# Strassen's seven products for the output layer of the last eight token tiles, in a fused retention and MLP kernel

## Chip, cores, metric

One Trainium2 chip, one core. The metric is the device time of one launch in microseconds (us), median of several runs. TensorE is PE in the profile (PEld: its weight loads), VectorE DVE, ScalarE ACT, GpSimd POOL, SyncE SP.

## The reference

Two layers follow each other. The first is a linear recurrence per batch and head with decay `gamma`; the second an MLP over all 4 x 768 = 3072 tokens with `d_model` 512 and `d_ff` 2048:

```python
for t in range(S):                      # S = 768, 4 batches, 8 heads of 64
    state = gamma * state + k[:, :, t]^T v[:, :, t]
    y[:, :, t] = scale * q[:, :, t] state
x = y as (3072 tokens, 512)
h = x @ w_in                            # 512 -> 2048
g = h + sin(alpha * h) ** 2 / (alpha + 1e-9)
out = g @ w_out                         # 2048 -> 512
```

## The kernel before

The recurrence is done in 24 chunks of 128 tokens (token tiles); a chunk's results land transposed, in bf16, in `xT`. The tiles go through the MLP in ten groups of sizes 4, 2, 2, 2, 2, 2, 2, 2, 2, 4 (`sizes`; group 0 is the first). Where a group is called g below, it is numbered 0 to 9.

The first layer of a group works in slots (class `Slot`): four matmuls with K = 128 for each block f of 128 of the 2048 hidden units write `ph` in PSUM; ScalarE takes the sine (L613) and squares it (L618), VectorE forms `s * rec_alpha + ph` (L625, `add`) and writes it in bf16 to `gT`. A group of two tiles has slots of two blocks (128x256 each, 8 slots); group 9, with four tiles, has slots of one block (128x512, 16 slots). The second layer (`ff_out`, L635) multiplies a tile's 16 blocks of `gT` by `w_out`: 16 matmuls of 512 columns into one bank `po`, which VectorE copies to SBUF (`take`, L649) and SyncE stores.

The order on each engine is the order of the code (a manual schedule). `phase(g, outs, att, ...)` writes one group: per slot n, in this order, the slot's matmuls with sine and square; what is left of the previous recurrence step (`exit`: `xT` from `py`, L494; `keep`: the state `s_f`; `hand`: its copy `s_q`); the recurrence step placed at this slot (`att`: matmuls into `py` or `y`, scores into `pa`, then the mask on VectorE, L406); a share of `outs`, which are the output matmuls of group g-1; and last the slot's `add`. Slot (g, n) below is slot n of phase g. After phase 9 the outputs of group 9 stand alone: three tiles by `ff_out`, the fourth by `last_tile`.

```python
for g in range(2, NG):
    phase(g, out_pieces(g - 1, range(sizes[g - 1])), atts[g], 4 // sizes[g], ...)
for fn in out_pieces(NG - 1, range(sizes[-1] - 1)):
    fn()
last_tile(NG - 1, sizes[-1] - 1)
```

PSUM has eight banks, in three tags: `mm`, four buffers of one bank in rotation (slots, `po`, some scores); `two`, one buffer of two banks (`py`, `y`); `pa`, one buffer of two banks (scores; the slots (6, 5) and (7, 5) as well). A tile that takes a buffer waits for the last reader of the tile before it.

Of the kernel before, what the change touches and what calls it, by code (L numbers as in the profile page):

```python
# [38 lines left out]
def kernel(  # L39
# [91 lines left out]
    def load_seq(bt, names="qkv", part=slice(None), between=None):  # L131
# [3 lines left out]
        if ("seq", bt) not in raw:  # L135
            raw["seq", bt] = (big.tile([128, nh, 2, NP, D], BF16, name=f"qk_seq{bt}"),
                              big.tile([128, nh, NP, D], BF16, name=f"v_seq{bt}"))
# [502 lines left out]
    def take(g, ts, by=None):  # L640
        o_sb = work.tile([128, d_model], F32, name="o_sb", tag="o_sb", bufs=5)
        if (g, ts) == end:
            h = d_model // 2
            nc.vector.tensor_copy(o_sb[:, :h], po[g, ts][:, :h])
            nc.scalar.copy(o_sb[:, h:], po[g, ts][:, h:])
        elif by is nc.scalar:
            nc.scalar.copy(o_sb, po[g, ts])
        else:
            nc.vector.tensor_copy(o_sb, po[g, ts])  # L649
# [2 lines left out]
        for r in (half(0), half(1)) if g == NG - 1 else (slice(0, 128),):
            nc.sync.dma_start(out=out_view[r, groups[g][ts], :], in_=o_sb[r])

    def last_tile(g, ts):

        lo = 0
        for n in (3 * d_model // 4, d_model // 4):
            c = slice(lo, lo + n)
            lo += n  # L660
            ph = psum.tile([128, n], F32, name="poh", tag="mm", bufs=4)
            for f in range(FF):
                nc.tensor.matmul(ph, gT[g][:, f, ts * C:(ts + 1) * C], w_out[:, f, c],  # L663
                                 start=(f == 0), stop=(f == FF - 1))
            o_sb = work.tile([128, d_model], F32, name="o_sb", tag="o_sb", bufs=5)[:, :n]
            if lo < d_model:
                nc.scalar.copy(o_sb, ph)  # L667
            else:
                nc.vector.tensor_copy(o_sb, ph)
            nc.sync.dma_start(out=out_view[:, groups[g][ts], c], in_=o_sb)  # L670
# [225 lines left out]

    def last_loads():
        nc.gpsimd.tensor_copy(seen, st["qkT", P[17]][:, 0, 0:1])
# [41 lines left out]
```

## Time and profile before

| | |
|---|---|
| time, median of 3 runs | 207.42 us (207.19 to 208.68) |
| profiled execution, span | 207.1 us |
| PE busy | 200.0 us, 97% of the span |
| DVE, ACT, POOL busy | 154.5, 151.9, 123.1 us (75, 73, 59%) |
| matmuls | 2383 |
| chain that ended last | PE 85%, DMA 7%, POOL 6% |

The profile gives one execution. Its groups of instructions name source line, engine, output and inputs, shapes and a count, with busy time and mean duration. The timeline has start and duration, and in brackets how long the engine had waited before and for whom. Windows are stretches of the span with each engine's busy time. An engine's instructions overlap a little: the step from one start to the next is what it can repeat.

### The profile page before, as it was taken

The page shows a single profiled execution, that of the slowest core. Times are in us where ns is not written, and L with a number is a line of the kernel's source. Part 1 is how long each engine was busy: PE and PEld are TensorE (multiplying, and loading weights), DVE is VectorE, ACT ScalarE, POOL GpSimd, SP SyncE. Part 2 cuts the span into 40 slices and gives each one's busy share as a digit, 9 for nine tenths or more (in the row PEclk, how much of TensorE's full clock was granted, in tenths as well). Part 3 has the DMA queues.
Part 4 walks back from the last instruction along what each step waited for, and adds up shares of the span by engine and source line. Part 5 has one row for each costly group of instructions (what it writes and reads, how often), then busy time and mean ns, then how long its engine had stood idle before and what let it go on. Part 6 is the DMA issues. An engine that isn't in the chain of part 4 may idle for free.

```text
span 207.1 us, 5839 instructions
## 1 busy us (share of the span) xinstructions
PE 200.0 (97%) x2383; PEld 124.8 (60%) x2383; DVE 154.5 (75%) x324; ACT 151.9 (73%) x310; POOL 123.1 (59%) x171
## 2 busy tenths in 40 slices
PE   7889999999989999999999999999999999999994
PEld 7435544557766766666766666766766654444443
DVE  4777499977999888878889695985977965656220
ACT  7768788657997787787787869688686779999000
POOL 8998986999999976899692916974220000000000
DMA  8999999999999999999997896994714101010223
GB/s 128 145 175 191 201 201 176 167 128 112 224 152 184 95 166 179 171 129 128 203 146 69 105 125 118 120 120 108 104 42 64 53 1 52 0 54 0 88 64 101
DMA packets 102810, 24.79 MB, mean 120 GB/s; under 512 B 93392, under 2 KB 99840, under 8 KB 102784
## 3 DMA queue, kind: packets, MB, share of 16 engines
q0 software_dynamic: 80080, 13.38, 93.6%
q1 hardware_dynamic: 22704, 11.06, 28.0%
q8 instruction: 18, 0.29, 0.6%
q14 instruction: 8, 0.07, 0.1%
HBM read 27.30 MB, written 6.29 MB: 162 GB/s over the span
## 4 chain that ended last, share of the span: by engine, by line
PE 85%; DMA 7%; POOL 6%; issue 0%; DVE 0%; POOLq 0%
PE po L635 38%; PE ph L610 38%; DMA w_out<-in_moe_w_out_dram 4%; DMA qkT<-qkr 3%; POOL qkr L125 3%; POOL vr L125 2%; PE poh L663 2%; PE py L372 1%; PE pt L290 1%; PE pa L387 1%; PE py L436 1%; POOL w_in L161 1%; PE py L445 1%; PE pa L394 1%; PE pa L420 1%; PE y L436 1%
## 5 line engine op out<-in xcount | busy, mean ns | idle before, releaser
L625 DVE SCALAR_TENSOR_TENSOR gT<-s,rec_alpha,ph 128x256 bf16<-128x256 f32 (+3 forms) x164 | 79.6, 522 | 27.9 <-ACT s L618 27.5
L610 PE MATMUL ph<-xT,w_in 128*128 128x256 bf16 (+3 forms) x656 | 98.3, 291 | 0.0
L613 ACT ACTIVATE s<-ph,alpha_sb 128x256 f32<-128x256 f32 (+3 forms) x164 | 76.0, 506 | 28.2 <-PE ph L610 24.7
L635 PE MATMUL po<-w_out,gT 128*128 128x512 bf16 x368 | 94.7, 380 | 0.1
L610 PEld LDWEIGHTS <-w_in 128*128 128x128 bf16 x656 | 63.2, 98 | 32.6 <-DVE s_f L568 0.5
L618 ACT ACTIVATE s<-s 128x512 f32<-128x512 f32 (+1 forms) x94 | 58.7, 625 | 2.8
L635 PEld LDWEIGHTS <-gT 128*128 128x128 bf16 x368 | 34.3, 98 | 30.2 <-DVE gT L625 0.5
L149 POOL DMA_DIRECT2D qk_seq<-in_q_dram x32 | 21.5, 704 | 4.1 <-DMA v_seq<-in_v_dram 3.9
L149 POOL DMA_DIRECT2D qk_seq<-in_k_dram x32 | 21.3, 703 | 3.6 <-DMA qk_seq<-in_q_dram 2.9
L649 DVE COPY o_sb<-po 128x512 f32<-128x512 f32 x20 | 13.8, 688 | 9.2 <-PE po L635 8.8
L149 POOL DMA_DIRECT2D v_seq<-in_v_dram x24 | 16.8, 754 | 0.0
L188 POOL TENSOR_TENSOR v_seq<-v_seq,kgq 128x512 bf16<-128x512 bf16 x9 | 9.3, 1060 | 5.9 <-DMA v_seq<-in_v_dram 5.9
L125 POOL DMA_DIRECT2D vr<-in_v_dram x11 | 10.3, 932 | 1.6 <-DMA w_in<-in_moe_w_in_dram 1.1
L406 DVE TENSOR_TENSOR aTw<-pa,maskq 128x768 bf16<-128x768 f32 x10 | 9.5, 953 | 0.0
L667 ACT COPY o_sb<-poh 128x384 f32<-128x384 f32 x1 | 0.5, 479 | 12.0 <-PE poh L663 12.0
L494 DVE TENSOR_TENSOR xT<-py,qg 128x512 bf16<-128x512 f32 x13 | 8.9, 683 | 0.5 <-PE py L452 0.5
L682 PE MATMUL spare<-warm 128*128 128x112 bf16 (+1 forms) x54 | 7.8, 316 | 1.2 <-DVE warm L198 1.2
L520 POOL CAST s_q<-s_f 128x256 bf16<-128x256 f32 x1 | 0.4, 396 | 14.2 <-DVE s_f L514 14.2
L390 DVE TENSOR_TENSOR aT<-pa,mask 128x1024 bf16<-128x1024 f32 x7 | 8.5, 1219 | 0.1
L520 ACT CAST s_q<-s_f 128x256 bf16<-128x256 f32 x12 | 4.7, 394 | 2.7 <-DVE s_f L514 2.7
L125 POOL DMA_DIRECT2D qkr<-in_q_dram x7 | 6.4, 918 | 0.3 <-DMA w_out<-in_moe_w_out_dram 0.3
L161 POOL DMA_DIRECT2D w_in<-in_moe_w_in_dram x8 | 6.2, 792 | 0.7 <-DMA w_out<-in_moe_w_out_dram 0.6
(123 smaller groups left out, 175.5 us busy)
## 6 DMA issues: line engine op xcount, KB each, us to landing
out_dram<-o_sb SPq DMA_DIRECT2D x20, 256.0 KB, 4.2
w_in<-in_moe_w_in_dram POOLq DMA_DIRECT2D x8, 256.0 KB, 8.6
w_out<-in_moe_w_out_dram POOLq DMA_DIRECT2D x8, 256.0 KB, 8.3
vr<-in_v_dram POOLq DMA_DIRECT2D x11, 128.0 KB, 5.6
v_seq<-in_v_dram POOLq DMA_DIRECT2D x16, 80.0 KB, 6.2
qkr<-in_q_dram POOLq DMA_DIRECT2D x7, 128.0 KB, 6.3
qkr<-in_k_dram POOLq DMA_DIRECT2D x7, 128.0 KB, 6.2
qk_seq<-in_q_dram POOLq DMA_DIRECT2D x16, 48.0 KB, 4.9
```

The lines of the kernel that those rows point to most:

```text
L125: nc.gpsimd.dma_start(out=t, in_=chunk_of(src, j))
L149: nc.gpsimd.dma_start(out=o, in_=src[bt, head(b, m, e), now[0] * C:(now[-1] + 1) * C, :].rearrange("(f i) d -> i f d", i=64))
L188: eng.tensor_mul(t, t, by[:, j % NCH, :, None].to_broadcast([128, H, D]))
L390: return {"mask": lambda: nc.vector.tensor_mul(aT.rearrange("p e n t -> p (e n) t"), pa.rearrange("p e (n t) -> p (e n) t", n=NP), mask_bc)}
L406: return {"mask": lambda: nc.vector.tensor_mul(aT, pa[:, :, 0:384].rearrange("p e (m t) -> p e m t", m=2), maskq[:, None, None, :].to_broa ...
L494: nc.vector.tensor_mul(o, st["pyw", old][:, :, 0:256].rearrange("p b (m t) -> p b m t", m=2), by)
L610: nc.tensor.matmul(self.ph[:, m, :], w_in[:, i, f * 128:(f + 1) * 128], xT[g][:, i, self.lo:self.hi], start=(m == 0 and i == 0), stop=(i = ...
L613: nc.scalar.activation(out=self.s[:, m, :], in_=self.ph[:, m, :], func=ACTF.Sin, scale=alpha_sb[:, f:f + 1])
L618: nc.scalar.activation(out=self.s, in_=self.s, func=ACTF.Square)
L625: nc.vector.scalar_tensor_tensor(gT[self.g][:, f, self.lo:self.hi], self.s[:, m, :], rec_alpha[:, f:f + 1], self.ph[:, m, :], op0=ALU.mult ...
L635: nc.tensor.matmul(po[g, ts], gT[g][:, f, ts * C:(ts + 1) * C], w_out[:, f, :], start=(f == 0), stop=(f == FF - 1))
L649: nc.vector.tensor_copy(o_sb, po[g, ts])
```

## The change

The output layer of group 7, group 8 and the two halves of group 9 (`fast = (7, 8, 9)`) is now computed for a pair of tiles at once, as a product of 2x2 blocks: two tiles by two halves of the hidden units, times two halves of the hidden units by two halves of the output columns. Strassen's scheme needs seven block products in place of eight. Each is 8 matmuls of 256 columns (K = 128 each), so a pair has 56 matmuls of 256 columns where it had 32 of 512.

The combined blocks are made in bf16. Those of `w_out` (`mix_w`, five combinations, 20 pieces of 128x512): 8 pieces on GpSimd, 12 on VectorE behind slots of phases 6 and 7. Those of `gT` (`mix_g`): a sum, a difference and a third sum for each pair of blocks j and j+8, behind a slot; for group 7 the first two on GpSimd and the third on VectorE, for group 8 all on GpSimd, for group 9 all on VectorE. So that j and j+8 come together, the slots of these groups take their blocks in that order. Class `Seven` holds a pair: products 5 and 2 go into bank `b`, 4 and 3 and later 7 and 6 into bank `a`, 1 into bank `c`. ScalarE copies `b` to SBUF (`hold`, `b_sb`); VectorE adds `a` and `b_sb` (`cross`: two of the four output blocks), forms `t_sb` = `c` - `b_sb` (`rest`) and adds it to `a` (`main`: the other two). The stores are 128x256.

```diff
-            self.g, self.fs = g, range(f, f + nf)
+            self.g, self.fs = g, f if isinstance(f, tuple) else range(f, f + nf)
...
+    def mix_w(eng, count=1):
+        for _ in range(count):
+            n, i = w_todo.pop(0)
+            a, b, op = W_MIX[n]
+            js = slice(2 * i, 2 * i + 2)
+            w_mix[n, i] = next(w_home)
+            eng.tensor_tensor(w_mix[n, i], w_block(*a, js), w_block(*b, js), op=op)
...
+        engs[0].tensor_tensor(ts, s0, s1, op=ALU.add)
+        engs[1].tensor_tensor(td, d0, d1, op=ALU.subtract)
+        engs[2].tensor_tensor(tx, x0, x1, op=ALU.add)
...
+        IN = {5: "b", 2: "b", 4: "a", 3: "a", 1: "c", 7: "a", 6: "a"}
...
+        def hold(self):
+            self.bsb = self.tmp("b_sb")
+            nc.scalar.copy(self.bsb, self.at["b"])
...
+        def banks(k):
+            if g < NG - 2:
+                if k == "c":
+                    return psum.tile([128, 2, 512], F32, name="c", tag="two")[:, 0, 0:NH]
+                return psum.tile([128, 2, NH], F32, name=k, tag="mm", bufs=4)
+            if k == "c":
+                return psum.tile([128, 2, 512], F32, name="c", tag="pa")[:, 0, 0:NH]
+            if "ab" not in po:
+                po["ab"] = psum.tile([128, 2, 512], F32, name="ab", tag="two")
+            return po["ab"][:, "ba".index(k)].rearrange("p (x n) -> p x n", x=2)
+        s = Seven(g, 0, banks)
+        return s.pieces((5, J), (2, J), s.hold, (4, J), (3, J), s.cross, (1, J), s.rest, (7, J), (6, J), s.main)
...
+        def far_banks(k):
+            if k == "b":
+                return near_banks(k)
+            if k == "a3":
+                return psum.tile([128, 2, 512], F32, name="a3", tag="pa")
+            if "a4c" not in po:
+                po["a4c"] = psum.tile([128, 2, 512], F32, name="a4c", tag="two")
+            return po["a4c"][:, int(k == "c"), 0:NH]
+        x, y = Seven(g, 0, near_banks), Seven(g, 1, far_banks, True)
+        todo = x.pieces((5, J0), (2, J0), (4, J0), (3, J0), (5, J1), (2, J1), x.hold, (4, J1), (3, J1), x.cross, (1, J), x.rest)
+        todo += y.pieces((5, J), (2, J), y.hold, (4, J), (3, J), y.cross)
+        todo += x.pieces((7, J), (6, J), x.main)
+        todo += y.pieces((1, J), y.rest, (7, J), lambda: y.main(7), (6, J, 0), lambda: y.main(0), (6, J, 1), lambda: y.main(1))
...
+            if g in fast and (nf == 2 or n % 2):
+                mix_g(g, n if nf == 2 else n // 2, g_by[g])
+            for fn in behind_slot.get((g, n), ()):
+                fn()
+    g_by = {7: (nc.gpsimd, nc.gpsimd, nc.vector), 8: (nc.gpsimd,) * 3, 9: (nc.vector,) * 3}
...
     def last_loads():
+        mix_w(nc.gpsimd, 3)
         nc.gpsimd.tensor_copy(seen, st["qkT", P[17]][:, 0, 0:1])
         load_seq(3, "v")
+        mix_w(nc.gpsimd, 5)
...
+    for spot in ((6, 0), (6, 2), (6, 3), (6, 6), (6, 7), (7, 0), (7, 1), (7, 2), (7, 3), (7, 5), (7, 6), (7, 7)):
+        behind_slot.setdefault(spot, []).append(lambda: mix_w(nc.vector))
     for g in range(2, NG):
-        phase(g, out_pieces(g - 1, range(sizes[g - 1])), atts[g], 4 // sizes[g], tags=tags[g], early=(6,) if g == 5 else ())
-    for fn in out_pieces(NG - 1, range(sizes[-1] - 1)):
-        fn()
-    last_tile(NG - 1, sizes[-1] - 1)
+        outs = fast_pieces(g - 1) if g - 1 in fast else out_pieces(g - 1, range(sizes[g - 1]))
+        phase(g, outs, atts[g], 4 // sizes[g], tags=tags[g], early=(6,) if g == 5 else ())
+    fast_end(NG - 1)
```

`J` is range(8), `J0` its first seven and `J1` the last. `last_tile` is gone, and the last pair's `a` is split in two banks so that its end leaves in pieces of 128 columns.

**Place one: VectorE in phase 7, from the copy of `po` in the slot before it up to the mask of the recurrence step at slot (7, 4).** Before:

```order
L649 COPY o_sb<-po 128x512
L625 SCALAR_TENSOR_TENSOR gT<-s,rec_alpha,ph 128x256 x8
L649 COPY o_sb<-po 128x512
L625 SCALAR_TENSOR_TENSOR gT<-s,rec_alpha,ph 128x256 x2
L406 TENSOR_TENSOR aTw<-pa,maskq 128x768
L568 TENSOR_TENSOR s_f<-s_f,pa 128x256
```

Now, from the copy in slot (7, 3) on (L683 is `mix_w`, L717 the third sum of `mix_g`; the slots (7, 0) to (7, 2) have the same pair behind their adds):

```order
L645 COPY o_sb<-po 128x512
L626 SCALAR_TENSOR_TENSOR gT<-s,rec_alpha,ph 128x256 x2
L717 TENSOR_TENSOR g_mix<-gT 128x128
L683 TENSOR_TENSOR w_mix<-w_out 128x512
L407 TENSOR_TENSOR aTw<-pa,maskq 128x768
L569 TENSOR_TENSOR s_f<-s_f,pa 128x256
```

Two instructions have come behind each slot's adds, and ahead of the mask and of `s_f`; GpSimd makes the other two combinations (L715, L716, 128x256 each) of the same slot at the same time.

**Place two: VectorE around the recurrence step at slot (8, 4), from that step's mask on.** Before:

```order
L406 TENSOR_TENSOR aTw<-pa,maskq 128x768
L625 SCALAR_TENSOR_TENSOR gT<-s,rec_alpha,ph 128x256 x2
L494 TENSOR_TENSOR xT<-py,qg 128x2x2x128
L514 TENSOR_TENSOR s_f<-s_f,pa 128x256
L625 SCALAR_TENSOR_TENSOR gT<-s,rec_alpha,ph 128x256 x4
```

Now (L782 is `cross`, L788 `rest`):

```order
L407 TENSOR_TENSOR aTw<-pa,maskq 128x768
L782 TENSOR_TENSOR o_sb<-a,b_sb 128x512
L626 SCALAR_TENSOR_TENSOR gT<-s,rec_alpha,ph 128x256 x2
L495 TENSOR_TENSOR xT<-py,qg 128x2x2x128
L515 TENSOR_TENSOR s_f<-s_f,pa 128x256
L788 TENSOR_TENSOR t_sb<-c,b_sb 128x512
L626 SCALAR_TENSOR_TENSOR gT<-s,rec_alpha,ph 128x256 x4
```

TensorE at the same slot, in the changed kernel, where the share of output matmuls behind the recurrence step goes over from product 3 to product 1 (with the semaphores waited for):

```order
L761 LDWEIGHTS gT
L761 MATMUL a<-w_mix,gT 128x256
L761 LDWEIGHTS g_mix [waits DVE_49]
L761 MATMUL c<-w_mix,g_mix 128x256 [waits PE_49]
L761 LDWEIGHTS g_mix
```

The first matmul of product 1 is a wait that was not there: it opens `c` in the buffer `two`, which `py` of this slot's recurrence step holds until L495 has read it. L495 stands behind `cross` and behind the adds of slot (8, 4).

**Place three: TensorE in slot (9, 4), in the changed kernel, at the end of product 2 (`ab` holds the banks `b` and `a` of group 8 in one tile).**

```order
L611 MATMUL ph<-xT,w_in 128x512
L761 LDWEIGHTS g_mix
L761 MATMUL ab<-w_out,g_mix 128x256
L761 LDWEIGHTS gT
L761 MATMUL ab<-w_mix,gT 128x256 [waits Activation_49]
L611 LDWEIGHTS w_in
L611 MATMUL ph<-xT,w_in 128x512 [waits DVE_49]
```

ScalarE at the same place:

```order
L614 ACTIVATE s<-ph,alpha_sb 128x512
L619 ACTIVATE s<-s 128x512
L769 COPY b_sb<-ab 128x512
```

Product 4 now waits for `hold` (L769), which ScalarE does behind the sine and the square of slot (9, 4); before, no output matmul of this phase waited for ScalarE but through `gT`.

More of the change, by code (lines that the diff above doesn't have):

```diff
@@ L135, in load_seq @@
         if ("seq", bt) not in raw:
[L136 to L137 removed]
+            raw["seq", bt] = (big.tile([128, nh, 2, NP, D], BF16, name=f"qk_seq{bt}", tag=f"qk_seq{bt}"),
+                              big.tile([128, nh, NP, D], BF16, name=f"v_seq{bt}", tag=f"v_seq{bt}"))
         tqk, tv = raw["seq", bt]
@@ L629 @@
     po = {}
-    end = (NG - 1, sizes[-1] - 1)
     def ff_out(g, ts, f):
@@ L641, in take @@
         o_sb = work.tile([128, d_model], F32, name="o_sb", tag="o_sb", bufs=5)
[L642 to L646, printed above, removed]
+        if by is nc.scalar:
             nc.scalar.copy(o_sb, po[g, ts])
@@ L651, in take @@
             return o_sb
[L652 to L670, printed above, removed]
+        nc.sync.dma_start(out=out_view[:, groups[g][ts], :], in_=o_sb)
@@ new lines, with w_homes @@
+    w_todo = [(n, i) for n in (1, 4, 3, 7, 6) for i in range(FH // 2)]
+    def w_homes():
+        for _ in range(11):
+            yield big.tile([128, 2, NH], BF16, name="w_mix", tag="vr", bufs=11)
+        for tag, n in (("qk_seq1", 6), ("v_seq1", 3)):
+            t = big.tile([128, n, 2, NH], BF16, name="w_mix", tag=tag)
+            for i in range(n):
+                yield t[:, i]
+    w_home = w_homes()
+    def mix_w(eng, count=1):
[5 more added lines that the diff above has]
+            eng.tensor_tensor(w_mix[n, i], w_block(*a, js), w_block(*b, js), op=op)
@@ new lines, in fast_end, with near_banks @@
+    def fast_end(g):
+        J, J0, J1 = range(FH), range(FH - 1), range(FH - 1, FH)
+        def near_banks(k):
+            if k == "c":
+                return psum.tile([128, NH], F32, name="c", tag="mm", bufs=4)
+            return psum.tile([128, 2, NH], F32, name=k, tag="mm", bufs=4)
+        def far_banks(k):
[11 more added lines that the diff above has]
+        todo += y.pieces((1, J), y.rest, (7, J), lambda: y.main(7), (6, J, 0), lambda: y.main(0), (6, J, 1), lambda: y.main(1))
+        for fn in todo:
+            fn()
```

134 lines of the change are left out of this document (131 added, 3 removed).

## The prediction

> **What bounds the kernel now.** I read the busy time by windows first, cut at the phases, then the chain of waits, then the timeline of the places that the change touches. Windows (columns: stretch, its length, busy time of PE, PEld, DVE, ACT, POOL, granted clock):
>
> ```profile
> 137.60:152.90 15.30, 15.30 (x210) 10.53 (x209) 12.04 (x26) 11.75 (x25) 6.87 (x8) 1.00 0.68 84
> 152.90:169.48 16.58, 16.58 (x258) 11.29 (x257) 12.85 (x26) 11.97 (x26) 0.40 (x1) 1.00 0.24 50
> 169.48:190.20 20.72, 20.72 (x98) 9.40 (x97) 12.71 (x19) 19.99 (x33) 0.00 (x0) 1.00 0.07 26
> 190.20:204.30 14.10, 14.01 (x81) 7.14 (x79) 4.02 (x7) 1.56 (x3) 0.00 (x0) 1.00 0.30 74
> ```
>
> These are phases 7, 8, 9 and the end. TensorE fills all four at full clock, so a matmul less is time less, and a wait of TensorE is time more, one for one. ScalarE in phase 9 (19.99 of 20.72) and VectorE (12 to 13 of 15 to 20) are the next in line. The chain has the price of a matmul:
>
> ```profile
> 167.90 0.87 PE ph L610 x8
> ...
> 189.93 10.79 PE po L635 x50
> ...
> 204.25 0.29 DVE o_sb L669
> ```
>
> 256 columns take 0.87 / 8 = 0.109 us, 512 take 10.79 / 50 = 0.216: the rate is the same, nothing is lost on short matmuls.
>
> **The change, part by part.**
>
> *Saving.* A pair went from 32 x 0.216 = 6.91 to 56 x 0.109 = 6.09: 0.82 each, **-3.3** for four. The kernel stops as before, with a 128-column VectorE step and one store.
>
> *Prices of the new combinations.* Rows by shape:
>
> ```profile
> L188 DVE TENSOR_TENSOR vr<-vr,kg 128x512 bf16<-128x512 bf16 x7 | 4.7, 677 | 0.9 <-DMA vr<-in_v_dram 0.9
> ...
> L281 DVE COPY qkT<-pt 128x512 bf16<-128x512 bf16 x3 | 1.3, 421 | 1.4 <-PE pt L279 1.4
> ...
> L243 DVE COPY maskq<-maskq 128x64 bf16<-128x64 bf16 x1 | 0.2, 182 | 0.0
> L188 POOL TENSOR_TENSOR v_seq<-v_seq,kgq 128x512 bf16<-128x512 bf16 x9 | 9.3, 1060 | 5.9 <-DMA v_seq<-in_v_dram 5.9
> L577 POOL CAST s_q<-s_f 128x512 bf16<-128x512 f32 x2 | 1.2, 612 | 6.6 <-DVE s_f L572 6.6
> L520 POOL CAST s_q<-s_f 128x256 bf16<-128x256 f32 x1 | 0.4, 396 | 14.2 <-DVE s_f L514 14.2
> ```
>
> No row has two bf16 tensors on VectorE: 512 elements cost between 0.42 (L281, all operands of two bytes) and 0.68 (L188, whose table is f32). I take 0.42, as here all operands have two bytes, and by L281 and L243 about 0.28 for 256 and 0.21 for 128; less 0.08 of overlap between neighbours that is 0.34, 0.20 and 0.13. At L188's price it would be 0.60 and 0.33, and the sum 2.7 higher (below). The Trainium skill ("VectorE: DVE Perf Modes", "The perf-mode tier table") gives two-tensor operations on bf16 in SBUF twice the f32 rate; no run here shows it, and it agrees with the end that I took. On GpSimd a 256 is an estimate of 0.62 (L520 and L577 give 0.18 fixed; the rest of L188's 1.06 halved). The 8 pieces of `mix_w` on GpSimd, 3 and 5 of 1.06, lie in two of its waits, the 5.9 of the L188 row and this one:
>
> ```profile
> POOL seen L898 <- DMA qkT<-qk_seq: 3.8, 1, 3.8
> ```
>
> They cost nothing; without that cover it would be 8.5 of GpSimd, and `v_seq` late by as much.
>
> *Phase 6.* One `mix_w` (0.34) stands ahead of the mask of slot (6, 4), as in phase 7 below, where the slack is about 0.1: **+0.3**.
>
> *Phase 7.* VectorE and TensorE:
>
> ```profile
> 141.94 0.87 DVE L625 SCALAR_TENSOR_TENSOR gT<-s,rec_alpha,ph 128x256 bf16<-128x256 f32 x2 [0.86 <-ACT s L618]
> ...
> 145.41 0.87 DVE L625 SCALAR_TENSOR_TENSOR gT<-s,rec_alpha,ph 128x256 bf16<-128x256 f32 x2
> 146.28 0.96 DVE L406 TENSOR_TENSOR aTw<-pa,maskq 128x768 bf16<-128x768 f32 x1
> 147.16 0.41 DVE L568 TENSOR_TENSOR s_f<-s_f,pa 128x256 f32<-128x256 f32 x1
> ...
> 147.68 1.04 PE L610 MATMUL ph<-xT,w_in 128*128 128x256 bf16 x8
> ...
> 152.02 0.87 DVE L625 SCALAR_TENSOR_TENSOR gT<-s,rec_alpha,ph 128x256 bf16<-128x256 f32 x2 [0.27 <-ACT s L618]
> ...
> 153.09 0.69 DVE L649 COPY o_sb<-po 128x512 f32<-128x512 f32 x1 [0.19 <-PE po L635]
> ...
> 154.62 1.04 PE L610 MATMUL ph<-xT,w_in 128*128 128x256 bf16 x8
> ```
>
> A plain slot leaves VectorE 0.86 free; slot (7, 3) leaves nothing, the mask follows its adds at once, and `s_f` ends at 147.57, when slot (7, 5), which takes the buffer `pa`, starts at 147.68. So what VectorE adds up to there is TensorE's wait. Per slot it adds 0.05 (an estimate, for the wait on its own result) + 0.21 + 0.34 = 0.6: hidden in three slots, bare at the fourth. But GpSimd works on its two combinations in the same moment, and one place of the trace shows such a meeting:
>
> ```profile
> 30.83 0.69 DVE L620 TENSOR_TENSOR s<-s 128x512 f32<-128x512 f32 x1
> ...
> 35.25 1.79 DVE L620 TENSOR_TENSOR s<-s 128x512 f32<-128x512 f32 x1
> 35.43 1.05 POOL L252 TENSOR_TENSOR qg<-qg,step 128x512 f32<-128x512 f32 x1
> ```
>
> The same VectorE instruction took 1.10 longer, the length of the GpSimd one. The Trainium skill ("SBUF — State Buffer", "SBUF: two separate sides") says that VectorE with two SBUF inputs and a GpSimd operation lock each other out for a whole instruction; the three rows agree, and `mix_w` and `mix_g` are such instructions. Without the lock my sum is 2.9 lower. I take one lock-out of 0.62 per slot (`mix_w` behind GpSimd's sum; L717 starts first): 1.22, so 3 x (1.22 - 0.86) + 1.22 = 2.3 at slot (7, 5). Behind it, up to the copy L649 that frees a bank for slot (8, 1), VectorE adds 0.21 + 2 x 1.22 = 2.65; it has 0.27 + 0.19 free (the waits of its last two rows), and from the copy's end at 153.78 to that slot, 0.1 earlier than 154.62, another 0.7: 1.5 is left. **+3.8**. With no lock-out it is 0.6 + 0.3 = 0.9; with two per slot 4.8 + 3.4 = 8.2.
>
> *Phase 8.* Slot (8, 4) and the step behind it:
>
> ```profile
> 160.94 1.03 PE L610 MATMUL ph<-xT,w_in 128*128 128x256 bf16 x8
> 162.01 0.84 ACT L613 ACTIVATE s<-ph,alpha_sb 128x256 f32<-128x256 f32 x2 [0.24 <-PE ph L610]
> ...
> 162.62 1.04 PE L635 MATMUL po<-w_out,gT 128*128 128x512 bf16 x4
> ...
> 162.84 0.95 DVE L406 TENSOR_TENSOR aTw<-pa,maskq 128x768 bf16<-128x768 f32 x1
> ...
> 163.71 0.86 DVE L625 SCALAR_TENSOR_TENSOR gT<-s,rec_alpha,ph 128x256 bf16<-128x256 f32 x2
> ...
> 164.49 0.68 DVE L494 TENSOR_TENSOR xT<-py,qg 128x512 bf16<-128x512 f32 x1
> ...
> L647 ACT COPY o_sb<-po 128x512 f32<-128x512 f32 x3 | 1.7, 579 | 0.9 <-PE po L635 0.9
> ...
> L649 DVE COPY o_sb<-po 128x512 f32<-128x512 f32 x20 | 13.8, 688 | 9.2 <-PE po L635 8.8 <-ACT o_sb L647 0.4
> ```
>
> Count from the slot's start, 160.94. TensorE reaches its output matmuls at +1.68, and after four of 0.109 stands at product 1 at +2.1. Product 1 needs L494, which ended at +4.23; now `cross` (0.60, priced as L649 less overlap) stands ahead of it, and `hold` (0.58, L647) has pushed the sine of slot (8, 3), and with it the mask, some 0.3: +5.1. **TensorE waits 3.0.** With both hidden it is 2.2, since the way over sine, square, adds and L494 is there in any case. Behind TensorE's wait queue slots (8, 5) to (8, 7) and all that ScalarE and VectorE do with them. Slot (8, 4) also waits for `hold` to free its bank: `hold` stands behind sine, square and a state copy of slot (8, 2), whose way on ScalarE (1.07 + 0.87 + 0.54 + 0.34 + 0.58 = 3.4 from that slot's start) is as long as two of TensorE's slots (2 x 1.63); I take 0.2, and 0.1 for slot (9, 0) and the last L494. **+3.3**.
>
> *Phase 9.* One of its slots:
>
> ```profile
> 187.61 1.03 PE L610 MATMUL ph<-xT,w_in 128*128 128x512 bf16 x4
> ...
> 188.67 0.69 ACT L613 ACTIVATE s<-ph,alpha_sb 128x512 f32<-128x512 f32 x1
> ...
> 189.39 0.63 ACT L618 ACTIVATE s<-s 128x512 f32<-128x512 f32 x1
> ...
> 190.05 0.75 DVE L625 SCALAR_TENSOR_TENSOR gT<-s,rec_alpha,ph 128x512 bf16<-128x512 f32 x1 [0.55 <-ACT s L618]
> 190.72 0.68 DVE L649 COPY o_sb<-po 128x512 f32<-128x512 f32 x1
> ```
>
> Product 4 in slot (9, 4) waits for `hold`: 1.06 from its start to the sine, 0.72 to the square, 0.55 on (0.63 less the overlap), 0.58 for `hold` and 0.05 for the signal: 2.96; TensorE is there at 0.87 + 2 x 0.109 = 1.08. **+1.9.** Slot (9, 5) is queued behind, and ScalarE waits for that in turn, so nothing gives it back. ScalarE can repeat a slot in 0.72 + 0.55 = 1.27, TensorE will take 4 x 0.216 + 3.5 x 0.109 = 1.25: level, so ScalarE takes perhaps 0.2 of the saving and no more. VectorE: two adds of 0.67 and the mixes 0.34 + 3 x 0.20 + 0.1 make 2.4 in 2 x 1.25, and `cross`, `rest`, `main` (3 x 0.60) come on top: over the eleven slots behind `hold` that is 5.5 x 2.4 + 1.8 = 15.0 in 13.7, so it ends 1.3 late, 1.5 with the waits on single results. Undelayed, the first sum of the last slot (15) is ready 1.06 + 1.27 + 0.67 + 0.5 = 3.5 after that slot's start, and `J1` asks for it after 0.87 + 4 x 0.109 + 28 x 0.109 = 4.35. Of the 1.5 this covers 0.85; `main` of group 8, which stands between the last adds, takes 0.35 of the cover away: **+1.0** ahead of the end.
>
> *The end.* `a4` and `c` of the last pair share a tile, and product 7 waits until `rest` has read `c`: 0.16 + 0.65 + 0.07, **+0.9**. In the same way the last 128 columns wait for the step on the 128 before them: 0.16 + 0.29 + 0.07, **+0.5**.
>
> *Sum.* -3.3 + 0.3 + 3.8 + 3.3 + 1.9 + 1.0 + 0.9 + 0.5 = **+8.4**, on the profiled span of 207.1: 215.5. The median is 0.3 above that span, so 215.8.
>
> **The rivals.**
>
> *No lock-out:* the L620 row is one event, and GpSimd's issue may fall between VectorE's. Then 2.9 less: 212.9. *Two lock-outs per slot* (for it: in the L620 row VectorE started first and lost): 4.4 more, 220.2. *VectorE mixes at L188's rate:* in phase 9 a pair of slots then costs 3.0 of 2.5, over five pairs 2.7 more, 218.5.
>
> *Faster:* matmuls alone decide. Price: -3.3, less the 0.3 + 0.9 of phases 6 and 7, gives 205.3; it needs the four waits on `two`, `ab` and the split bank (3.3, 1.9, 0.9, 0.5) and VectorE's delay to vanish. It decides where the reader of `py` is done 2.1 after the slot's start; against it, the way over sine, square, adds and L494 took 4.2 in the trace, and three further reads lie behind the waits. *The waits are real but half as long,* because the work behind them gives some back: without lock-out 207.4 + 5.5 - 3.3 = 209.6. *The seven products don't take less* speaks against the chain's 0.87 and 0.86 rows: ruled out.
>
> **How the numbers follow.** One lock-out per slot 0.40 (215.8), no lock-out 0.22 (212.9), two 0.12 (220.2), slow mixes 0.08 (218.5), half waits 0.13 (209.6), faster 0.05 (205.3). The likeliest gives 215.8. The range 209.5 to 219.0 leaves out the faster case and most of the two lock-outs. A measurement of this kernel tells 1% (2.1) from no change: faster 0.05, same 0.06 (the lower half of the half waits), slower 0.89.
>
> **What the profile after would show.** PE idle of about 3 us at the first product-1 matmul of phase 8, ended by VectorE's L495; about 1.9 in slot (9, 4), ended by L769; 0.9 and 0.5 in the last 4 us. L717 or L683 on VectorE lengthened to GpSimd's L715 beside them, and a wait of slot (7, 5) for L569; if they run 0.2 and 0.4 long, the lock-out is wrong and phase 7 costs under 1. L710 at 0.42 or 0.68 settles the rate. Busy PE must fall by 3.3. The forecast is wrong if PE goes through product 1 without waiting, for then a new order on VectorE hides what I called exposed.

## Result, and the profile after

The changed kernel takes **218.64 us** (median of 4 runs, 217.97 to 219.34), the kernel before 207.58 us beside it: ratio 1.050, 95% interval 1.044 to 1.056. It is slower by 11.1 us as the difference of the medians, and by 10.3 us by the ratio (0.0498 x 207.6); the experiments below are given by their ratios. Ratios leave out executions more than 1.5% above the fastest of their kernel, and where the profiled execution is one of these, the text says so.

The span of the profiled execution is 216.4 us. The time stands 1.9 to 2.0 us above the span of the same execution, here and in each run of the kernel before that stood beside the experiments (205.2 to 207.7 us of span for 207.2 to 209.7 us of time). So the profile of before, with a span of 207.1, belongs to one of the slower executions; by the medians of before beside the runs (207.6 to 208.2) a typical one has 205.6 to 206.2. For comparing stages I therefore use the kernel `layout_only` (below), which is the kernel before with the change's tile layout, at 206.1 us. Windows of it and of the changed kernel, cut where phases 7, 8 and 9 start (stretch, length, busy time of PE, PEld, DVE, ACT, POOL, granted clock, DMA share, GB/s):

```profile
0.00:136.66 136.66, 133.57 (x1743) 87.02 (x1744) 111.97 (x247) 106.41 (x227) 117.22 (x164) 1.00 1.62 153
136.66:151.96 15.30, 15.30 (x209) 10.53 (x208) 12.04 (x27) 11.76 (x25) 5.65 (x7) 1.00 0.41 77
151.96:168.55 16.59, 16.59 (x258) 11.30 (x257) 12.86 (x27) 12.00 (x26) 0.40 (x1) 1.00 0.23 50
168.55:206.10 37.55, 34.73 (x177) 16.56 (x175) 16.96 (x25) 21.55 (x35) 0.00 (x0) 1.00 0.17 50
```
```profile
136.75:155.34 18.59, 15.66 (x208) 10.68 (x209) 18.07 (x39) 11.77 (x25) 13.63 (x19) 1.00 0.48 69
155.34:176.90 21.56, 18.08 (x282) 14.27 (x281) 16.07 (x34) 12.32 (x27) 15.78 (x26) 0.92 0.14 38
176.90:216.40 39.50, 33.02 (x246) 22.76 (x247) 27.12 (x63) 22.13 (x37) 2.78 (x6) 1.00 0.14 48
```

Up to phase 7 nothing is lost (0.1 us). Phase 7 is 3.29 longer, phase 8 4.97, phase 9 with the end 1.95; with the 0.1 that is the 10.3 between the spans. TensorE is no longer busy throughout: it idles 2.9 of the 18.6 us of phase 7 and 3.5 of the 21.6 of phase 8, and in phase 8 its granted clock is 0.92. VectorE has become nearly full in phase 7 (18.07 of 18.59).

The waits of TensorE behind this, from the timeline of PE:

```profile
147.07 0.25 PE L395 MATMUL pb<-qkT 64*64 64x128 bf16 x3 [1.29 <-DVE o_sb L645]
...
147.85 1.02 PE L635 MATMUL po<-w_out,gT 128*128 128x512 bf16 x3 [0.29 <-DVE gT L626]
150.12 1.05 PE L611 MATMUL ph<-xT,w_in 128*128 128x256 bf16 x8 [1.24 <-DVE s_f L569]
...
157.85 1.03 PE L611 MATMUL ph<-xT,w_in 128*128 128x256 bf16 x8 [0.60 <-DVE o_sb L645]
...
165.67 0.61 PE L761 MATMUL a<-w_mix,gT 128*128 128x256 bf16 x4
169.16 0.82 PE L761 MATMUL c<-w_mix,g_mix 128*128 128x256 bf16 x3 [2.88 <-DVE xT L495]
169.77 1.92 PE L611 MATMUL ph<-xT,w_in 128*128 128x256 bf16 x8
...
184.81 0.27 PE L761 MATMUL ab<-w_mix,gT 128*128 128x256 bf16 x1 [1.69 <-ACT b_sb L769]
...
202.49 0.39 PE L761 MATMUL b<-w_out,g_mix 128*128 128x256 bf16 x2 [0.40 <-DVE g_mix L710]
...
210.89 1.03 PE L761 MATMUL a4c<-w_mix,g_mix 128*128 128x256 bf16 x8 [0.78 <-DVE t_sb L788]
211.76 0.61 PE L761 MATMUL a<-w_mix,g_mix 128*128 128x128 bf16 x8
212.75 0.61 PE L761 MATMUL a<-w_mix,g_mix 128*128 128x128 bf16 x8 [0.38 <-DVE o_sb L802]
```

The bracket leaves out the drain of the matmul before it: from the end of issue of the four `a` matmuls (165.67 + 4 x 0.109 = 166.11) to 169.16 are 3.05 us. And eight matmuls that take 1.04 elsewhere took 1.92 right behind this wait. The windows of the wait and of what follows:

```profile
165.67:169.16 3.49, 0.61 (x13) 0.31 (x5) 3.49 (x8) 1.03 (x3) 3.02 (x6) 0.99 0.15 48
169.16:172.54 3.38, 3.38 (x16) 2.39 (x17) 0.27 (x1) 0.82 (x2) 1.44 (x4) 0.50 0.10 33
```

For 3.4 us behind the wait TensorE ran at half clock and lost 1.7 us. The other three executions have the same mean clock, 0.992; 1.7 us are 0.008 of their spans.

In phase 7, VectorE beside GpSimd (timelines of DVE and POOL):

```profile
138.41 0.56 DVE L683 TENSOR_TENSOR w_mix<-w_out 128x512 bf16<-128x512 bf16 x1
...
140.26 1.52 DVE L717 TENSOR_TENSOR g_mix<-gT 128x128 bf16<-128x128 bf16 x1
...
142.94 0.22 DVE L717 TENSOR_TENSOR g_mix<-gT 128x128 bf16<-128x128 bf16 x1
143.09 0.89 DVE L683 TENSOR_TENSOR w_mix<-w_out 128x512 bf16<-128x512 bf16 x1
143.90 0.86 DVE L626 SCALAR_TENSOR_TENSOR gT<-s,rec_alpha,ph 128x256 bf16<-128x256 f32 x2
144.79 0.80 DVE L717 TENSOR_TENSOR g_mix<-gT 128x128 bf16<-128x128 bf16 x1
145.51 0.90 DVE L683 TENSOR_TENSOR w_mix<-w_out 128x512 bf16<-128x512 bf16 x1
```
```profile
140.42 0.66 POOL L715 TENSOR_TENSOR g_mix<-gT 128x256 bf16<-128x256 bf16 x1
141.04 0.66 POOL L716 TENSOR_TENSOR g_mix<-gT 128x256 bf16<-128x256 bf16 x1
142.99 0.70 POOL L715 TENSOR_TENSOR g_mix<-gT 128x256 bf16<-128x256 bf16 x1 [1.29 <-DVE gT L626]
143.66 0.85 POOL L716 TENSOR_TENSOR g_mix<-gT 128x256 bf16<-128x256 bf16 x1
```

L717 takes 0.22 where it starts ahead of GpSimd's sum (142.94), and 1.52 where GpSimd was at work when it started (140.26): it ended behind both sums. `w_mix` takes 0.89, and L716 beside it 0.85 for 0.66. In phase 6, where GpSimd only issues DMAs, `w_mix` took this:

```profile
125.07 0.42 DVE L683 TENSOR_TENSOR w_mix<-w_out 128x512 bf16<-128x512 bf16 x1
```
Two L626, which read `ph` from PSUM, keep their 0.86 to 0.87 in both phases.

### The profile page after: what moved, and what is told of

The parts are those of the page before. It is cut to its first block, busy times and chain, and to the rows that moved or that the text cites. A ratio compares the mean times of both kernels' runs of the same rounds, so it can differ in the third digit from the quotient of the medians.

```text
span 216.4 us, 6144 instructions
## 1 busy us (share of the span) xinstructions
PE 198.2 (92%) x2453; PEld 134.3 (62%) x2479; DVE 174.2 (80%) x383; ACT 152.9 (71%) x313; POOL 157.1 (73%) x219
## 4 chain that ended last, share of the span: by engine, by line
PE 64%; DVE 16%; DMA 7%; POOL 6%; ACT 4%; issue 3%; ACTq 0%; POOLq 0%
PE ph L611 29%; PE po L635 21%; DVE gT L626 6%; DMA qkT<-qkr 3%; DMA w_out<-in_moe_w_out_dram 3%; PE a L761 2%; POOL qkr L125 2%; DVE w_mix L683 2%; ACT s L614 2%; POOL vr L125 2%; PE b L761 1%; PE a4c L761 1%; PE c L761 1%; PE py L373 1%; DVE g_mix L717 1%
## 5 line engine op out<-in xcount | busy, mean ns | idle before, releaser
L626 DVE SCALAR_TENSOR_TENSOR gT<-s,rec_alpha,ph 128x256 bf16<-128x256 f32 (+3 forms) x164 | 79.3, 521 | 18.5 <-ACT s L619 17.2
L635 PE MATMUL po<-w_out,gT 128*128 128x512 bf16 x236 | 62.7, 379 | 2.3 <-issue 1.6
L635 PEld LDWEIGHTS <-gT 128*128 128x128 bf16 x256 | 23.7, 98 | 18.9 <-DVE gT L626 0.5
L149 POOL DMA_DIRECT2D qk_seq<-in_q_dram x32 | 21.6, 713 | 3.5 <-DMA v_seq<-in_v_dram 1.9
L761 PEld LDWEIGHTS <-g_mix 128*128 128x128 bf16 x168 | 15.8, 100 | 10.4 <-DVE xT L495 3.2
L715 POOL TENSOR_TENSOR g_mix<-gT 128x256 bf16<-128x256 bf16 x16 | 10.8, 676 | 11.3 <-DVE gT L626 11.3
L716 POOL TENSOR_TENSOR g_mix<-gT 128x256 bf16<-128x256 bf16 x16 | 11.6, 724 | 0.0
L125 POOL DMA_DIRECT2D vr<-in_v_dram x11 | 10.3, 941 | 1.1 <-DMA w_in<-in_moe_w_in_dram 0.9
L189 POOL TENSOR_TENSOR v_seq<-v_seq,kgq 128x512 bf16<-128x512 bf16 x9 | 9.9, 1103 | 0.0
L645 DVE COPY o_sb<-po 128x512 f32<-128x512 f32 x13 | 8.9, 684 | 0.7 <-ACT o_sb L643 0.4
L495 DVE TENSOR_TENSOR xT<-py,qg 128x512 bf16<-128x512 f32 x13 | 8.9, 685 | 0.5 <-PE py L453 0.5
L683 POOL TENSOR_TENSOR w_mix<-w_out 128x512 bf16<-128x512 bf16 x8 | 9.0, 1200 | 0.0
L683 DVE TENSOR_TENSOR w_mix<-w_out 128x512 bf16<-128x512 bf16 x12 | 8.0, 668 | 0.0
```

The source lines that it names most:

```text
L149: nc.gpsimd.dma_start(out=o, in_=src[bt, head(b, m, e), now[0] * C:(now[-1] + 1) * C, :].rearrange("(f i) d -> i f d", i=64))
L189: eng.tensor_mul(t, t, by[:, j % NCH, :, None].to_broadcast([128, H, D]))
L626: nc.vector.scalar_tensor_tensor(gT[self.g][:, f, self.lo:self.hi], self.s[:, m, :], rec_alpha[:, f:f + 1], self.ph[:, m, :], op0=ALU.mult ...
L635: nc.tensor.matmul(po[g, ts], gT[g][:, f, ts * C:(ts + 1) * C], w_out[:, f, :], start=(f == 0), stop=(f == FF - 1))
L683: eng.tensor_tensor(w_mix[n, i], w_block(*a, js), w_block(*b, js), op=op)
L715: engs[0].tensor_tensor(ts, s0, s1, op=ALU.add)
```

## Experiments

All come from the changed kernel, save `layout_only`. Where a state copy moves to ScalarE (`three_banks` and its variant, `groups_8_9` and its variant), the line numbers shown are one lower. Ratios are to the kernel before on the same chip; "us" is (ratio - 1) x 207.6, so that all stand on one footing (the changed kernel: +10.3).

| kernel | ratio (95% interval) | us |
|---|---|---|
| changed kernel | 1.050 (1.044 to 1.056) | +10.3 |
| layout_only | 1.001 (0.998 to 1.004) | +0.2 |
| no_gpsimd_7 | 1.033 (1.025 to 1.041) | +6.8 |
| c_in_mm | 1.038 (1.032 to 1.043) | +7.8 |
| bc_and_end | 1.040 (1.033 to 1.046) | +8.2 |
| three_banks | 1.021 (1.016 to 1.025) | +4.3 |
| three_banks_no_gpsimd_7 | 1.010 (1.006 to 1.013) | +2.0 |
| groups_8_9 | 1.022 (1.017 to 1.027) | +4.6 |
| groups_8_9_apart | 0.999 (0.996 to 1.002) | -0.2 |
| group_9 | 0.994 (0.991 to 0.997) | -1.3 |
| one_meeting | 0.992 (0.989 to 0.995) | -1.7 |
| stall_short | 0.999 (0.996 to 1.002) | -0.2 |
| stall_long | 1.003 (0.999 to 1.006) | +0.5 |

**layout_only**: the kernel before with three edits of the change that set only the homes of tiles.

```diff
-raw["qk", j] = big.tile([128, 2, H, D], BF16, name="qkr", tag="qkr", bufs=9)
+raw["qk", j] = big.tile([128, 2, H, D], BF16, name="qkr", tag="qkr", bufs=10)
...
-        raw[name, 0] = big.tile([128, H, D], BF16, name=f"{name}b")
+        raw[name, 0] = raw["qk", 0][:, "qk".index(name)]
```

> The kernel before with the change's tile layout alone (first q and k in a tenth buffer of qkr, tags on qk_seq and v_seq), no Strassen product and no combination. Theory: nothing, 207.5 us, and the time stands 0.3 us above the span as before. Rival: the layout brings the 1.0 us by which the first six phases ended earlier in the profile after, and the extra 1.7 us that the time after stood above its span.

Measured: 208.05 us to 207.71, no difference. The layout costs nothing, and the step between time and span is 2.0 here too: it isn't the change's.

**c_in_mm**: product 1 of group 7 away from `py`'s tile.

```diff
-return psum.tile([128, 2, 512], F32, name="c", tag="two")[:, 0, 0:NH]
+return psum.tile([128, NH], F32, name="c", tag="mm", bufs=4)
```

> Group 7's product 1 is written to a bank of mm in place of the tile two. Theory (the 2.88 us wait is for L495, which reads py in that tile, and the 1.7 us of half clock behind it follow from the wait): both go, a few tenths come back at product 7, which waits for cross; 4.0 to 4.5 us less, 214.3 us, and the granted clock is 1.00. Rival (half clock has another cause): only the wait goes, 215.8 us, with clock 0.99. Second rival (TensorE would stand a step later for the same chain of sine, square and adds): under 1.5 us less.

Measured: 2.5 us less by the ratios, not 4.0 to 4.5. In its profile the wait and the half clock behind it are gone, and phase 8 is 3.9 shorter (17.62 us for 21.56), though a new wait of 1.07 has come in, for the state copy L521, which stood behind GpSimd's sums. But the clock was not 1.00: 0.992, 0.992 and 0.998 in the executions of the ratio (0.008 of 214 us is 1.7 us lost, one stretch of 3.4 us at half clock), and 0.984 in the profiled one, which is the longest and not in the ratio. Its phase 7 shows where: one `w_mix` took 2.94 beside GpSimd, VectorE's list ran late from there on, TensorE waited 2.03 for a copy further down that list, and the clock was halved (timeline of DVE, windows):

```profile
139.68 2.94 DVE L683 TENSOR_TENSOR w_mix<-w_out 128x512 bf16<-128x512 bf16 x1
```
```profile
145.31:149.42 4.11, 2.08 (x91) 1.67 (x90) 4.08 (x8) 2.15 (x5) 3.95 (x5) 0.98 0.12 25
149.42:155.85 6.43, 6.00 (x48) 2.91 (x47) 5.79 (x14) 1.43 (x3) 3.37 (x5) 0.50 0.34 82
```

At half clock the 6.0 us of work in the second window lost 3.0. So product 1's wait and the half clock behind it go together, as the theory had it, and phase 7 can have a half clock of its own. That it is phase 7 that lowered the clock in the executions of the ratio too is not shown, as they have no profile.

**bc_and_end**: `a` of group 8 gets a tile of its own, `b` and `c` share one; `c` of the last pair goes to `mm`.

```diff
+            if k == "a":
+                return psum.tile([128, 2, 512], F32, name="a", tag="two")[:, 0].rearrange("p (x n) -> p x n", x=2)
...
+                po["bc"] = psum.tile([128, 2, 512], F32, name="bc", tag="pa")
...
-            if k == "b":
+            if k in ("b", "c"):
                 return near_banks(k)
```

> Group 8's b and c share a tile in place of a and b, and the last pair's c has a bank of mm, apart from a4. Theory: the waits of 1.69 us (for hold, slot (9, 4)) and 0.78 us (for rest, last product 7) go, 2.5 us less, 216.1 us. Rival (ScalarE is level with TensorE in phase 9, so the time comes back as a wait for sine and square): 1 us less or nothing, 217.6 us or more.

Measured: 2.1 less, as the theory says within the interval. Its profile is of an execution of 407 us and isn't read. Two of its other three executions have a clock of 0.983, lower than the changed kernel's 0.992, so that the waits themselves may have been worth more than 2.1. The same edits in `three_banks` show where it comes from: phase 9 with the end takes 37.18 us there, 39.50 in the changed kernel, and neither the wait for `b_sb` nor the one for `t_sb` is left.

**no_gpsimd_7**: group 7's sums and differences on GpSimd left out; four of its products take `gT` instead.

```diff
+        if g != 7:
+            engs[0].tensor_tensor(ts, s0, s1, op=ALU.add)
+            engs[1].tensor_tensor(td, d0, d1, op=ALU.subtract)
```

> Phase 7 without its GpSimd combinations: the sums and differences of group 7 (L715, L716) are left out, and its products 5, 2, 7 and 6 take gT instead; everything that VectorE does in phase 7 (L717 and w_mix) stays. Lock-out theory: the VectorE rows shrink to 0.21 and 0.42, and of TensorE's waits in phase 7 and before slot (8, 1), 1.29 + 0.29 + 1.24 + 0.60 = 3.4 us, about 0.9 is left: some 2.5 us less, 216.1 us. Rival, VectorE is simply overloaded by 12 more instructions: the rows and the waits stay, 218.6 us.

Measured: 3.5 less by the ratios, with a wide interval; its profile is of an execution at clock 0.75 and isn't read. It was done again on a cleaner base:

**three_banks** and **three_banks_no_gpsimd_7**: `c_in_mm` and `bc_and_end` together, with the state copy L521 on ScalarE; and the same without group 7's sums on GpSimd.

```diff
-            copy = nc.gpsimd.tensor_copy if now // NCH == 3 else nc.scalar.copy
-            copy(s_q(now, now % NCH + 1), s_f(now))
+            nc.scalar.copy(s_q(now, now % NCH + 1), s_f(now))
```

> All tile changes together (c of group 7 in mm; b and c of group 8 in one tile; c of the last pair in mm), and the state cast L521 of phase 8 on ScalarE, for which TensorE waited 1.07 us behind GpSimd's combinations in c_in_mm. Theory (the waits are separate terms): 218.6 less 4.5 for product 1 and its half clock, less 2.5 for hold and rest, 211.6 us; what is left above 207.7 is phase 7 (3.4 us of waits) and 0.8 us at the end, less the saving. Rival (a wait taken away reappears on ScalarE or VectorE): 214 us or more.

> The same, and group 7's sums and differences on GpSimd are left out (its products 5, 2, 7 and 6 take gT instead). Lock-out theory: 2.5 us less than three_banks, 209.1 us; L717 and w_mix on VectorE take 0.22 and 0.42 throughout phase 7, and TensorE waits under 1 us there. Rival (VectorE overloaded in any case): as three_banks, 211.6 us.

Measured: 212.36 and 210.15 us. The three waits add up nearly as separate terms: 6.1 less than the changed kernel by the ratios (6.3 by the medians), 7.0 expected. Without GpSimd's sums it is 2.2 less again, 2.5 expected. Windows of phases 7, 8 and 9 with the sums, then of phase 7 without them:

```profile
137.07:155.50 18.43, 15.77 (x210) 10.68 (x209) 18.29 (x39) 11.76 (x25) 13.48 (x19) 1.00 0.42 66
155.50:173.22 17.72, 16.43 (x282) 13.52 (x281) 15.97 (x34) 12.53 (x28) 15.37 (x25) 1.00 0.17 47
173.22:210.40 37.18, 33.03 (x250) 22.77 (x247) 27.10 (x63) 21.99 (x37) 2.83 (x6) 1.00 0.15 50
```
```profile
137.09:153.73 16.64, 15.68 (x209) 10.55 (x208) 16.50 (x38) 11.75 (x25) 5.39 (x6) 1.00 0.64 77
```

Phase 7 falls from 18.43 to 16.64 us, with what VectorE has to do unchanged. TensorE's waits from there to slot (8, 1), with the sums and without (waited for: us, times, longest):

```profile
PE ph L610 <- DVE s_f L568: 1.2, 1, 1.2
PE pb L395 <- DVE o_sb L644: 1.1, 1, 1.1
PE po L634 <- DVE gT L625: 0.3, 1, 0.3
```
```profile
PE ph L610 <- DVE s_f L568: 0.8, 1, 0.8
PE ph L610 <- DVE o_sb L644: 0.3, 1, 0.3
```
The third sum takes 0.22 and `w_mix` 0.42 there, apart from two `w_mix` of 1.38 and 1.46 in the first three us and one third sum of 0.97: beside these GpSimd still ran `v_seq` or a state copy. What is left, 16.64 - 15.30 = 1.3, I put down to these three and to VectorE's plain load; no run tells them apart.

**groups_8_9**: group 7 as before; the seven `w_mix` of phase 7 on GpSimd; the tiles of `bc_and_end`, with the last product in one piece of 256 columns; L521 on ScalarE.

```diff
-    fast = (7, 8, 9)
+    fast = (8, 9)
...
-        behind_slot.setdefault(spot, []).append(lambda: mix_w(nc.vector))
+        behind_slot.setdefault(spot, []).append(lambda e=nc.vector if spot[0] == 6 else nc.gpsimd: mix_w(e))
```

> Seven products for groups 8 and 9 only (three pairs); group 7's output as before; the seven w_mix of phase 7 on GpSimd, which has no g_mix there, so that VectorE and GpSimd never combine in the same moment; a and bc apart, the last pair's c in mm, the last product in one piece, L521 on ScalarE. Theory: the saving of 3 x 0.82 = 2.5 us stays, less 0.2 in phase 6 and 0.4 ahead of the end: 2 us below before, 205.8 us. Rival (the third sum chain on GpSimd in phase 8, or ScalarE in phase 9, holds TensorE up): 207 us or more.

Measured: +4.6 us. The theory failed, and not by the rival. The profile is of a longer execution (216.0 us of span) than the two of the ratio (210.7 and 211.3), so its sizes aren't theirs; it shows where to look. Timelines of DVE and POOL:

```profile
138.05 7.20 DVE L682 TENSOR_TENSOR w_mix<-w_out 128x512 bf16<-128x512 bf16 x1
```
```profile
137.92 0.62 POOL L577 CAST s_q<-s_f 128x512 bf16<-128x512 f32 x1
138.50 1.04 POOL L189 TENSOR_TENSOR v_seq<-v_seq,kgq 128x512 bf16<-128x512 bf16 x1
139.50 2.24 POOL L682 TENSOR_TENSOR w_mix<-w_out 128x512 bf16<-128x512 bf16 x2
141.71 1.03 POOL L189 TENSOR_TENSOR v_seq<-v_seq,kgq 128x512 bf16<-128x512 bf16 x1
142.71 2.24 POOL L682 TENSOR_TENSOR w_mix<-w_out 128x512 bf16<-128x512 bf16 x2
```

One `w_mix` of 0.42 on VectorE ended only when seven GpSimd instructions, back to back, were through, and TensorE waited 5.9 us for the copy queued behind it. That this is the cause of the 4.6 us is tested next.

**groups_8_9_apart**: two more `w_mix` go from VectorE to GpSimd; the three left lie where GpSimd only issues DMAs.

```diff
-    for spot in ((6, 0), (6, 2), (6, 3), (6, 6), (6, 7), (7, 0), ..., (7, 7)):
+    for spot in ((6, 0), (6, 2), (6, 3), (7, 0), ..., (7, 7), (8, 0), (8, 1)):
```

> groups_8_9 with the last two w_mix of phase 6 taken from VectorE: three of the twelve late w_mix on VectorE in slots (6, 0), (6, 2) and (6, 3), where GpSimd only issues DMAs, the other nine on GpSimd in phases 7 and 8. Theory (in groups_8_9 one w_mix on VectorE took 7.20 us, because GpSimd ran seven instructions back to back beside it, and the 5.88 us wait of TensorE came from that): the wait goes, 205.8 us. Rival (three pairs load GpSimd and ScalarE too much): 208 us or more.

Measured: 208.06 us, the same as before. The wait is gone and phases 7 and 8 cost 0.3 us: the two `w_mix` beside GpSimd's chain were the cause. But the gain expected on three pairs isn't there. Phase 9 (window), then the last pause of VectorE in it and its last sum, then TensorE's waits behind the slots:

```profile
168.55:188.70 20.15, 20.05 (x120) 11.76 (x121) 18.01 (x43) 19.42 (x33) 3.19 (x6) 1.00 0.08 27
```
```profile
177.71 0.75 DVE L625 SCALAR_TENSOR_TENSOR gT<-s,rec_alpha,ph 128x512 bf16<-128x512 f32 x1 [0.45 <-ACT s L618]
...
192.28 0.43 DVE L709 TENSOR_TENSOR g_mix<-gT 128x512 bf16<-128x512 bf16 x1
```
```profile
189.79 1.05 PE L760 MATMUL b<-w_out,g_mix 128*128 128x256 bf16 x8 [0.31 <-DVE g_mix L709]
...
192.77 0.39 PE L760 MATMUL b<-w_out,g_mix 128*128 128x256 bf16 x2 [0.40 <-DVE g_mix L709]
```

TensorE is busy for 20.05 of the 20.15 us, and the 16 slots end 19.96 us after their start (188.07 + 4 x 0.109 = 188.51), for 20.72 before: the 0.82 of the third pair is nearly all there. It is lost again behind the slots. VectorE has no pause from 177.71 on, its last sums come late, and TensorE waits for them 0.31 and 0.40, or 0.48 and 0.57 with the drain. ScalarE, 19.42 us busy, is almost without a pause as well, but no wait of TensorE there ends with it.

**group_9**: seven products for group 9 alone, at the end; eleven of the late `w_mix` on GpSimd in phases 7 and 8; the end as in `groups_8_9`.

```diff
-    fast = (7, 8, 9)
+    fast = (9,)
...
+    for spot in ((6, 0), (7, 0), (7, 3), (7, 5), (7, 6), (7, 7), (8, 0), (8, 1), (8, 2), (8, 3), (8, 6), (8, 7)):
+        behind_slot.setdefault(spot, []).append(lambda e=nc.vector if spot[0] == 6 else nc.gpsimd: mix_w(e))
```

> Seven products for the last group only (two pairs, all in the end); eleven of the twelve late w_mix on GpSimd in phases 7 and 8, where nothing else combines. Theory: the saving of 2 x 0.82 = 1.6 us, less 0.4 for the last sum: 1.2 us below before, 206.5 us. Rival (VectorE, with the copies of group 8 and the combinations of group 9 in phase 9, is late for the end by more than the saving): 208 us.

Measured: 206.63 us to 208.17, faster by 0.7% (0.3 to 1.0%): better than the kernel before and than the changed one. Phases 7 and 8 take 15.29 and 16.59 us, as in `layout_only`; phase 9 with the end 36.58 for 37.55.

**one_meeting**: `group_9` with one `w_mix` given back to VectorE while GpSimd runs a chain.

```diff
-lambda e=nc.vector if spot[0] == 6 else nc.gpsimd: mix_w(e)
+lambda e=nc.vector if spot in ((6, 0), (7, 6)) else nc.gpsimd: mix_w(e)
```

> group_9 with one single w_mix of the chain in phase 8 moved to VectorE, behind slot (7, 6), while GpSimd runs its other w_mix and v_seq back to back from about 148.6 to 157. If VectorE is kept out for one GpSimd instruction, that row takes at most 1.06 + 0.42 = 1.5 us and the time stays at group_9's 206.6 us. If it is kept out until GpSimd's chain ends, the row takes 3 to 4.5 us, TensorE waits about 2 us for VectorE's copy, and the time is 208.5 us or more.

Measured: 206.40 us, no loss. The row, and GpSimd's beside it:

```profile
151.15 1.31 DVE L683 TENSOR_TENSOR w_mix<-w_out 128x512 bf16<-128x512 bf16 x1
```
```profile
149.90 3.57 POOL L683 TENSOR_TENSOR w_mix<-w_out 128x512 bf16<-128x512 bf16 x3
```

It ended at 152.46, late by less than one GpSimd instruction, while these three ran on to 153.47 and the chain behind them to 156.70. So a meeting costs between one instruction (here) and a chain of them (7.20, 2.94, 1.52). In the long cases a `v_seq` or a state copy was running or just starting when VectorE's instruction started, but so it was at 138.41 in the changed kernel, where `w_mix` took 0.56; what decides was not settled.

**stall_short** and **stall_long**: `group_9` with three and five unused copies on VectorE ahead of the last sum.

```diff
+                for _ in range(k):
+                    nc.vector.tensor_copy(junk, gT[g][:, 0])
```

> group_9 with three extra copies on VectorE (their result is not used) ahead of the very last sum, on which TensorE waits: an idle gap of about 1.5 us in the end, worked out from 3 x 0.6 less the 0.25 by which that sum was early. If a short gap leaves TensorE's clock alone, the time is 1.5 us above group_9, 208.1 us, with clock 1.00; if any gap halves the clock for some 3 us, 209.7 us, with clock 0.99.

> The same with five copies: a gap of about 2.7 us, near the 2.88 us after which the changed kernel's clock was halved. If the gap alone does it, the granted clock is about 0.99 in every run and the time 2.7 + 1.6 us above group_9, 210.9 us; if the burst around product 1 had a part in it, the clock stays 1.00 and the time is 209.3 us.

Measured: the copies took 0.45 each, not 0.6, so the gaps are 0.71 and 1.64 us, and the times 1.1 and 1.9 us above `group_9`. The clock stayed at 1.00 behind both in the profiles; one execution of `stall_short`, without a profile and outside the ratio, has 0.992 and 214.21 us. The gap of the second:

```profile
195.94 0.39 PE L765 MATMUL b<-w_out,g_mix 128*128 128x256 bf16 x2 [1.64 <-DVE g_mix L714]
```

A gap of 1.64 us left the clock alone. Behind one of 2.88 it was halved in the profile of the changed kernel, whose other runs have the same mean of 0.992, and behind 2.03 in phase 7 in that of `c_in_mm`. A gap near 2.7 was meant and not reached, so whether the gap alone does it at that length stays open.

## Why the prediction was right, and where it was off

The forecast of slower, by the waits it named, held; 215.8 us was 2.8 below the measured time, which lies close to the upper end of the range, 219.0. By the ratio the change costs 10.3 us, where 8.4 was forecast. Term by term:

- *Base.* "0.3 above that span" was wrong: the time stands 2.0 above its own span, and the profile of before was one of the slower executions. The sum was put on the right median all the same.
- *Saving, -3.3.* Right: the matmuls of `b`, `a` and `c` run at 0.109 each, and with two pairs and hardly a wait `group_9` kept 0.97 of its 1.64. The sign named for it, busy PE down by 3.3, can't be read off: the profile after shows 20 matmuls fewer than `layout_only` ahead of phase 7 (1723 for 1743), where both kernels have the same ones, so some records are missing, and half clock and drains count as busy.
- *Phase 6, +0.3.* 0.1 by the start of phase 7; `w_mix` ran in 0.42, as assumed.
- *Phase 7, +3.8.* 3.29 in the phase and 0.88 ahead of slot (8, 1) (156.21 + 7 x 0.109 = 156.97 to 157.85): 4.2. The lock-out was right, as were its victims; without GpSimd's sums 2.2 us go. That the sum came so near is in part luck: slot (7, 5) is 3.29 late (2.3 predicted), slot (8, 1) 0.88 more (1.5 predicted). Not foreseen was that TensorE takes part of it earlier: the copy L645, behind the `w_mix` of slot (7, 3), frees a bank that `pb` needs, 1.29 us. And "one per slot" was a mean of what lies between less than one and a whole chain.
- *Phase 8, +3.3.* The wait for L495 was 3.05 (predicted 3.0), and it was L495. **The step that failed stands behind it: that a wait costs its own length.** Behind this one the clock was halved for 3.4 us, which cost 1.7 more, a term that the sum doesn't have. It is the larger part of the miss.
- *Phase 9, +1.9 for `hold`.* 1.69 in the bracket, 1.85 with the drain. Right. *VectorE late, +1.0:* 0.40 at product 5's last piece, 0.57 with the drain, and 0.2 in the 14 matmuls of `b` before (1.72 us from their start to the next, for 1.53): about 0.8, so VectorE kept up a little better than the sum said.
- *The end, +0.9 and +0.5.* 0.78 and 0.38, each 0.17 more with the drain. Right. With the saving as priced, the measured terms add up to 9.8 of the 10.3.
- *Mixes at L188's rate* (the rival at 218.5): out. L710 takes 0.42, and the time of 218.6 near it is a coincidence. *Half waits* and *faster* are out as well. So is *two lock-outs per slot*, by the 4.2 of phase 7; its price was a slip, though: 0.21 + 2 x 1.84 less the free 0.27 + 0.19 + 0.7 is 2.7 and not 3.4, which makes it 219.5 and not 220.2.

The Trainium skill's "SBUF — State Buffer" ("SBUF: two separate sides"), on which the lock-out leaned, says that whichever of the two engines starts first holds the shared ports for its whole instruction. `one_meeting` agrees (1.31). The 7.20 row goes beyond it: VectorE didn't get in between GpSimd's instructions. The Trainium skill's "TensorE: Matmul & The Clock Gate" ("What's actually happening") has half clock after an idle window of about 3.4 us, judged in free-running windows; the 3.38 us at 0.50 fit such a window's length, but the gap ahead of it was 2.9 to 3.05, so a window that is only mostly idle is enough here. In windows of 0.1 us the half clock lasts from 169.11 to 172.53 in the changed kernel, from 149.26 to 156.09 in `c_in_mm` and from 144.64 to 151.47 in `groups_8_9`: once and twice 3.41 us.

## What to carry to other kernels

Before fewer matmuls are bought with additions, look which engine makes them and what it runs beside: on VectorE and GpSimd together, instructions with two SBUF inputs took turns, and one of 0.42 us took up to 7.20. A product that accumulates in a tile waited here for every reader of that tile, so put into one tile only what is read and written in the same order; three such tiles cost some 6 us here (`three_banks`), and moving them took no extra instruction. The seven products paid only at the end, where nothing else ran on GpSimd (0.7% for two pairs); with a third pair in phase 9, where the combinations leave VectorE no pause, the gain was lost to VectorE's last sums.

## What the runs showed of the hardware that was not expected

- A wait of TensorE can cost more than its length: behind 2.88 us of idle time stood 3.4 us at clock 0.50, behind 2.03 and behind 5.88 (`groups_8_9`) 6.8 us, the latter begun within the wait, behind 1.64 nothing. How idle the stretch ahead was doesn't decide alone: in the 3.41 us ahead of the half clock TensorE was busy for 0.58 (changed kernel), 1.54 (`c_in_mm`) and 0.00 us (`groups_8_9`), and in the changed kernel's phase 7 a stretch as long (146.70 to 150.11) with 1.46 us of work left the clock at 1.00.
- VectorE can be kept out by GpSimd for a whole chain: 7.20, 2.94 and 1.52 us for instructions of 0.42, 0.42 and 0.22; in other places for one instruction only.
- A VectorE instruction that reads one operand from PSUM (L626, two in 0.86) is not lengthened by GpSimd's sums.
- Two-tensor bf16 on VectorE, all in SBUF: 128x512 0.42, 128x256 0.28, 128x128 0.22 us; on GpSimd 1.1 to 1.25, 0.67 and 0.42.
